# Four sequences side by side in a linear-attention and feed-forward kernel: order of chunks, 64-token halves from the start, a new opening order, and the branch's registers

## The chip, the cores and the metric

One core of one Trainium2 chip. The metric is the device time of one execution in microseconds (us). The kernel before was timed three times: 488.36, 488.54 and 982.09 us; the median, 488.54 us, is the figure that the change is measured against. One further execution was profiled; it took 487.69 us, of which the trace covers a span of 485.9 us.

The engines are called by their short names in the profile: PE is the matrix engine (PEld is its weight load), DVE the vector engine, ACT the scalar engine, POOL the general-purpose engine (GpSimd), SP the engine whose queue issues most DMAs.

## The reference, cut to what matters

Two stages, chained. The first is a linear attention with a per-channel decay over 4 batches, 8 heads, 768 tokens and a head width of 48:

```python
state = np.zeros((B, H, D, D))
for t in range(S):
    cur = np.einsum('bhd,bhe->bhde', u[None] * kt, vt)
    y[:, :, t] = np.einsum('bhd,bhde->bhe', rt, state + cur)
    state = wt[:, :, :, None] * state + np.einsum('bhd,bhe->bhde', kt, vt)
```

The second takes the 3072 tokens (4 x 768) with 384 features each through a feed-forward layer of width 2048: `h = x @ w_in`, `g = h * sigmoid(1.702 h)`, `out = g @ w_out`, in float32. The four batches have nothing to do with each other; within a batch the state goes from token to token.

## The kernel before, in words

**Chunks.** The tokens are cut into 24 chunks of 128 (`NT`), six per batch, and taken in the order of memory: chunks 0 to 5 are batch 0, 6 to 11 batch 1, and so on. `chunk(t)` (line 406) is a generator that does one chunk in steps; each step is called for by a token of an order written by hand. In a chunk two prefix products of the decays are made by scans on DVE (L419, L425), r*k for the diagonal (L432), the scaled k and r (`kf`, `qf`, L440, L441); PE makes the diagonal terms `ps_d` (L448) and transposes `kf` (L474, or L468 later). The state of the chunk before is scaled on DVE (L459). Then, for chunks 0 to 5, the whole 128 x 128 chunk is done at once: the matrix `am` with the diagonal on it is written by ACT (L494, eight instructions), PE makes the state's update (L505, added on DVE in L511), the scores (L523) and the state's share of the output (L530; L568 in chunk 3), DVE puts the scores above the diagonal into `am` (L574), and PE multiplies with the values (L617; L613 in chunk 3). From chunk 6 on (`HALF`) `token_halves` (L316) does two halves of 64 tokens with an intermediate state `mid`: half the score columns, `am` by L349, the states by L354 to L359, L361 for the scores. There the matmuls are of 64 rows or columns, and `one_run` (L285) emits those of one chunk's outputs together with the scores and sums of the next chunk (`held`), except for the chunks in `ALONE`, 6 and 8, whose scores and sums run by themselves. The first chunk of a batch has no incoming state, the last makes no outgoing one.

**x.** The output of a chunk is written as a rounded high part by ACT and a remainder. For chunks 0 to 3 the remainder is made by a matmul with the matrix `minus` (L635) and an ACT copy (L636); later by DVE (L246). Rows of x are moved between partitions by `fill_x` (L645), six DMAs per group; of the first group, three chunks are moved so and chunk 3 is computed in the moved layout (L568, L613, with POOL copies L556, L562).

**Feed-forward.** Groups of four chunks (512 tokens); each group has 16 tasks, one per 128 columns of the width 2048, in all 96. A task is a first product (token `g`: nine matmuls), a gelu (`h`: two ACT instructions, one DVE subtraction, L693) and a second product (`y`: nine matmuls). The first 20 tasks use all 128 rows at once (L677, L707 to L709); tasks 20 to 94 are split by rows in two that run side by side (L733). The weights arrive as raw 64-bit words in 12 pieces (`fetch`, token `f`) and are converted in four steps (`convert`, token `w`: ACT L222 and L223; DVE L225 and L228; ACT L231; DVE L233).

**Order.** All engines take their instructions in program order. The first part is the string `RAMP` (L63): `l` loads a chunk, `a` does the next step of a chunk, `f`, `w`, `g`, `h`, `y` as above, `x` moves x, `k13` issues 13 matmuls on zeros (`keep_clock`, L713). `rest()` (L884) makes the order after it from the tables `PARTS`/`LATER`. DMAs are issued from SP's queue in `RAMP` and mostly from POOL's after it.

**End.** After the last task the sums in `acc` are compared with limits (L937 to L945); every engine loads the count (L948) and branches (L949) over a slow version of the whole kernel that runs only if a limit is broken. The output of a group is stored by three DMAs (`store`, L802).

Of the kernel before, what the change touches and what calls it, by code (L numbers as in the profile page):

```python
# [21 lines left out]
P = 128  # L22
# [30 lines left out]
PARTS = [("a", 0, 0), ("a", 1, 0), ("a", 2, 0), ("m", 2, 0), ("a", 2, 1), ("a", 3, 0), ("a", 3, 1), ("a", 5, 1),  # L53
         ("a", 5, 1), ("l", 5, 0), ("l", 5, 0), ("a", 5, 1), ("a", 5, 1), ("a", 8, 1), ("a", 8, 1), ("x", 8, 1)]
# [9 lines left out]
l0 M l0 a0 a0 a0 l0 k13 a0 a0 l1 l1 a0 a0 a1 k4 a0 a1 f2 a1 l1 a0 l2 a0 k1 a1 a1 a1 a1 a2 f2 k3 a0 a0 w2 a1 a1 a2 f0  # L64
a2 k1 a0 a1 a1 l3 l2 a2 a2 a2 k3 a1 a2 l3 a3 f0 a1 a2 a2 a2 w0 a3 f1 a3 a1 k2 a3 a2 f4 a3 w0 a3 k3 a2 a3 a3 a3 l4 a2
w0 a3 a3 a2 a4 f6 w0 a3 w2 x2 a3 w1 w1 k5 a3 k3 g0 f6 w2 g1 l4 w2 a4 h0 g2 f4 a4 w1 w1 h1 g3 w4 h2 w4 f3 a4 a4 a4 f8
y0 w3 f5 l5 g4 w3 h3 m4 l6 w4 a4 y1 w4 a4 w3 a4 g5 a5 w3 y2 a4 h4 a5 l5 a5 h5 y3 g6 w5 w5 m5 y4 a4 a5 w6 w6 h6 f7 w5
w5 w6 a5 w6 a6 g7 f8 w8 a5 y5 l6 w8 h7 g8 g9 w7 y6 a6 a6 a4 w7 a5 y7 w8 w8 a6 f10 h8 f9 u a5 a6 h9 w7 a6 a5 g10 w9
l7 f10 g11 a5 w7 a6 w9 l8 m6 a5 l7 a7 h10 y8 y9 w9 a6 w10 a7 g12 f11 w9 a6 y10 a7 h11 h12 a5 l9 w11 a7 w10 w11 a7 m7
a7 w10 a7 w11 y11 w10 y12 w11 a6 a7 g13 a7 a8 l8 h13 l9 g14 a6 a8 a8 g15 l10 a8 y13 h14 a7 m8 a7 a8 a8 h15 a9 a9 y14  # L70
a8 x7 y15 a8 a9 l10 a8 g16 g17 h16 m9 a9 h17 a9 a9 l11 g18 a9 y16 a10 a8 h18 y17 a9 g19 a10 a10 a8 a10 a9 a10 h19
m10 a10 l11
"""
WIDE = 512
CROSS = 6
HALF = 6
GAP = 3
ALONE = (HALF, 8)
# [10 lines left out]
def rwkv_ffn_kernel(ctx: ExitStack, tc, wkr, vp, vrk, ub, w_in, w_out, masks, vt, uc, out):  # L89
# [13 lines left out]

    hm = cp.tile([R2, 2 + H], F32, name="hm")
# [11 lines left out]
    after = cp.tile([P, C], F32, name="after")  # L116
# [31 lines left out]
    states = [at.tile([R2, TOP + NP * D], F32, tag=f"sf{i}", name="sf") for i in range(3)]  # L148
# [5 lines left out]
    loaded, state, pools, weighed, moves = {}, {}, {}, set(), []  # L154
# [8 lines left out]
    def load(t):  # L163
# [3 lines left out]
        loaded[t] = [a[0:R2], v]  # L167
        first, last = (TOP if t == 0 else 0), (R2 if t % (NT - 1) == 0 else P)
        rows = wkr.rearrange("t r w -> (t r) w")[t * R + first - TOP : t * R + last - TOP]
# [6 lines left out]
        else:  # L176
            for c0, n_ in ((1, n - 1), (n, NP * C), (n + NP * C, NP * C)):
                one, two = (slice(c0 + h * n_ // 2, c0 + (h + 1) * n_ // 2) for h in range(2))
                behind_moves(queue[0].dma_start(a[TOP:R2, one], wkr[t, :, one]))  # L179
                for h in range(2):  # L180
                    rows = slice(TOP + h * D, TOP + (h + 1) * D)
                    queue[0].dma_start(a[rows, two], wkr[t, (1 - h) * D : (2 - h) * D, two])  # L182
        yield
        assert t < 3 or t - 3 in weighed
        queue[0].dma_start(v[:, TOP:], vrk[t, :, 0:DM])
        if t >= WHOLE:
            rk = pools["late"].tile([P, 2 * DM], F32, tag="rk", name="rk_t")
            queue[0].dma_start(rk, vrk[t, :, DM:])
# [66 lines left out]
    def decays(t):  # L255
# [3 lines left out]
        queue[0].dma_start(w, wkr[t, :, 0 : n + 1])  # L259
# [793 lines left out]
```

## Time and profile before

| | us |
|---|---|
| median of three runs | 488.54 |
| profiled execution, device time | 487.69 |
| its span in the trace | 485.9 |
| first product's matmuls begin without break | 35.50 |
| last matmul begins | 479.11 |

PE is busy for 475.3 us of the span, 38 of its instructions being the `k` matmuls on zeros, all before 35 us. DVE is busy 60% of the span, ACT 53%, POOL 22%; DVE and ACT are much busier in the first quarter than later. The granted clock of PE is at full speed in every slice of the page but the last, in which no matmul runs. 48.47 MB are moved by DMA, at around 300 GB/s in the first 60 us and far less afterwards. An instruction's time in these views is from its start to its end; neighbours on one engine overlap a little, so where a sum is made along an engine, the distance from start to start counts.

### The profile page before, as it was taken

How to read it: one execution, taken by the hardware profiler on the slowest of the kernel's cores; microseconds unless marked ns; L12 is line 12 of the kernel's file. 1: busy time of each engine (PE TensorE's matmuls, PEld its weight loads, DVE VectorE, ACT ScalarE, POOL GpSimd, SP SyncE). 2: the span in 40 equal slices, each digit the busy share in tenths (PEclk: the TensorE clock that was granted, in tenths of full speed). 3: DMA queues.
4: the chain of work that ended last, by engine and by line, in shares of the span. 5: the costliest groups of instructions: out<-in, count | busy, mean ns of one | idle time of the engine just before them, and what ended most of it. 6: DMA issues, size and time to landing. Idle time of an engine off the chain costs nothing.

```text
span 485.9 us, 14346 instructions
## 1 busy us (share of the span) xinstructions
PE 475.3 (98%) x5915; PEld 405.7 (83%) x5915; DVE 289.6 (60%) x455; ACT 256.7 (53%) x611; POOL 107.5 (22%) x222
## 2 busy tenths in 40 slices
PE   7999999999999999999999999999999999999994
PEld 4768888888888888888888888888888888888873
DVE  7999999998866456556656566656575312121110
ACT  5888898875653534634544545445545432422222
POOL 4151000002232406433407334407200002100000
PEclk9999999999999999999999999999999999999998
DMA  8968954125522305223305234205220001100001
GB/s 298 318 234 308 313 170 152 48 93 145 163 75 74 99 3 132 102 70 109 97 5 148 75 94 115 87 14 131 72 63 2 3 1 34 67 2 1 1 0 71
DMA packets 20728, 48.47 MB, mean 100 GB/s; under 512 B 4816, under 2 KB 10032, under 8 KB 20656
## 3 DMA queue, kind: packets, MB, share of 16 engines
q1 hardware_dynamic: 12128, 26.72, 16.7%
q0 software_dynamic: 8128, 20.24, 14.9%
q8 instruction: 48, 0.79, 0.6%
q10 hardware_dynamic: 400, 0.53, 0.3%
q14 instruction: 24, 0.20, 0.1%
HBM read 40.49 MB, written 4.72 MB: 93 GB/s over the span
## 4 chain that ended last, share of the span: by engine, by line
PE 95%; DVE 2%; DMA 1%; issue 1%; ACT 0%; SPq 0%; ACTq 0%; PEldq 0%; DVEq 0%
PE po L733 31%; PE ph L733 30%; PE ph L677 9%; PE ps_c L293 5%; PE ps_a L293 3%; PE po L707 3%; PE po L709 3%; PE po L708 3%; PE ps_d L448 1%; PE ps_y L617 1%; PE ps_t L474 1%; PE ps_y L530 1%; PE ps_s L523 1%; PE ps_t L468 1%; DMA wkr_t<-in_wkr 1%; PE idle L722 1%
## 5 line engine op out<-in xcount | busy, mean ns | idle before, releaser
L733 PE MATMUL ph<-x,pair 64*128 64x512 f32 x1350 | 220.7, 377 | 0.0
L733 PE MATMUL po<-gh,pair 64*128 64x512 f32 x912 | 186.1, 383 | 0.2 <-SPq L738 0.2
L733 PEld LDWEIGHTS ph<-x,pair 64*128 64x128 f32 x1350 | 170.1, 186 | 17.8 <-ACT gf L692 0.6
L693 DVE TENSOR_TENSOR gl<-gf,gh 128x512 fp32r<-128x512 f32 x96 | 66.2, 691 | 147.8 <-ACT gf L692 147.8
L692 ACT ACTIVATE gh<-ph 128x512 fp32r<-128x512 f32 x84 | 49.9, 594 | 151.3 <-PE ph L733 144.3
L733 PEld LDWEIGHTS po<-gh,pair 64*128 64x128 f32 x912 | 113.5, 186 | 12.6 <-SPq L738 0.8
L733 PE MATMUL po<-gl,pair 64*128 64x512 f32 x456 | 117.1, 376 | 0.0
L733 PEld LDWEIGHTS po<-gl,pair 64*128 64x128 f32 x456 | 58.8, 186 | 5.7
L645 POOL DMA_DIRECT2D x<-x x33 | 16.7, 511 | 169.4 <-DVE x L246 77.1
L692 ACT ACTIVATE gf<-ph 128x512 f32<-128x512 f32 x84 | 49.6, 590 | 0.0
L677 PE MATMUL ph<-x,pair 128*128 128x512 f32 x189 | 45.5, 390 | 0.4 <-DMA x<-x 0.3
L677 PEld LDWEIGHTS ph<-x,pair 128*128 128x128 f32 x189 | 35.0, 188 | 7.9 <-DMA x<-x 1.0
L349 ACT ACTIVATE am<-eye,s 128x64 f32<-128x64 f32 x144 | 36.2, 336 | 3.8 <-PE ps_c L293 3.2
L182 POOL DMA_DIRECT2D wkr_t<-in_wkr x72 | 36.1, 505 | 5.5 <-issue 3.2
L419 DVE TENSOR_TENSOR_SCAN lp<-wkr_t,d1r 112x516 f32<-112x516 f32 x24 | 29.3, 1223 | 1.3 <-DMA wkr_t<-in_wkr 1.2
L246 DVE TENSOR_TENSOR x<-ps_c,x 112x512 fp32r<-112x512 f32 (+1 forms) x20 | 12.6, 638 | 29.2 <-ACT x L245 29.2
L425 DVE TENSOR_TENSOR_SCAN lp<-wkr_t,d1f 112x516 f32<-112x516 f32 x24 | 29.5, 1228 | 0.1
L245 ACT ACTIVATE x<-ps_c 112x512 fp32r<-112x512 f32 (+1 forms) x20 | 11.1, 555 | 29.4 <-PE ps_c L293 29.4
L293 PE MATMUL ps_a<-kq 48*64 48x64 f32 (+1 forms) x576 | 26.3, 221 | 0.0
L707 PE MATMUL po<-gh,pair 128*128 128x512 f32 x60 | 23.7, 396 | 0.0
L179 POOL DMA_DIRECT2D wkr_t<-in_wkr x36 | 18.8, 523 | 22.1 <-DVE lp L425 12.1
L709 PE MATMUL po<-gl,pair 128*128 128x512 f32 x60 | 23.2, 386 | 0.0
(128 smaller groups left out, 654.3 us busy)
## 6 DMA issues: line engine op xcount, KB each, us to landing
raw<-in_w_out SPq DMA_DIRECT2D x6, 1024.0 KB, 7.7
raw<-in_w_in SPq DMA_DIRECT2D x5, 1024.0 KB, 10.1
rk_t<-in_vrk POOLq DMA_DIRECT2D x12, 384.0 KB, 4.5
wkr_t<-in_wkr SPq DMA_DIRECT2D x4, 770.5 KB, 9.0
out_t<-ob POOLq DMA_DIRECT2D x12, 256.0 KB, 2.6
v_t<-in_vrk SPq DMA_DIRECT2D x12, 192.0 KB, 3.5
wkr_t<-in_wkr POOLq DMA_DIRECT2D x24, 96.0 KB, 2.6
wkr_t<-in_wkr POOLq DMA_DIRECT2D x48, 48.0 KB, 2.2
```

What stands on the lines that cost most here:

```text
L179: behind_moves(queue[0].dma_start(a[TOP:R2, one], wkr[t, :, one]))
L182: queue[0].dma_start(a[rows, two], wkr[t, (1 - h) * D : (2 - h) * D, two])
L293: mm = T.matmul(out, w, moving, start=start, stop=stop, skip_group_check=True)
L349: A.activation(am[h][:, p], eye, AF.Copy, scale=s[:, j : j + 1])
L419: V.tensor_tensor_scan(li.rearrange("r p c -> r (p c)")[:, ::-1], w1[:, ::-1], d1r.rearrange("r p c -> r (p c)")[:, ::-1], 0.0, op0=ALU.mu ...
L425: V.tensor_tensor_scan(pm.rearrange("r p c -> r (p c)"), w0, d1f.rearrange("r p c -> r (p c)"), 0.0, op0=ALU.mult, op1=ALU.add,)
L677: T.matmul(o, pair[w_], halves(x[:, x_, c, cs], plain), start=k_ == 0, stop=k_ == 3 * NM - 1)
L692: A.activation(g, ph, AF.Gelu_apprx_sigmoid, scale=1.0 / W_SCALE)
L693: V.tensor_tensor(gl, gf, gh.bitcast(F32), op=ALU.subtract)
L707: T.matmul(o, h_, halves(gh, plain), start=first, stop=False, skip_group_check=True)
L709: T.matmul(o, h_, halves(gl, plain), start=False, stop=f == NF - 1, skip_group_check=True)
L733: mm = T.matmul(by_twos(out), w[rows], halves(x[rows]), start=start, stop=stop, skip_group_check=True)
```

## The change

1. Chunk t now is chunk t // 4 of batch t % 4 (`place(t)` = t % B * CB + t // B): chunks 0 to 3 are the first of each batch, without incoming state; the state of chunk t comes from chunk t - 4; chunks 20 to 23 are the last. There are six state buffers instead of three, handed round by a table.
2. Chunks 0 to 2 go through `token_halves` in an `opening` form: scores in 64-token halves, only the first half's sums, `mid` copied by ACT, one output tile, remainder by PE as before (`by_tensor`). Chunk 3 has its own function `last_rows`. Their outgoing states are made later and separately (`first_state`, token `n`). Chunks 4 and 5 go through `token_halves` too (`CROSS` is 4, `ALONE` is 4 and 8).
3. In chunks 0 to 7 half of the diagonal matrices is written by POOL (`affine_select`) instead of ACT.
4. `RAMP` is another order; it has 33 matmuls on zeros before the first `g` and one after it instead of 38 and none.
5. The sums are compared during task 94, counted at task 95, and each engine loads the count ahead of the last store; the constants `eye` and `later` are made at the start instead of inside `RAMP`. The output of a group is stored as four pieces of 128 tokens per row, 512 bytes each, instead of one of 2 KB.

```diff
+    def place(t):
+        return t % B * CB + t // B
...
-        first, final = t % CB == 0, (t + 1) % CB == 0
+        opening, final = t < B, t >= NT - B
...
-            for b in range(1 if final else 2):
+            for b in range(1 if opening or final else 2):
...
-        if t in ALONE:
+        if opening or t in ALONE:
             one_run([], ahead)
...
+            if h and t < WHOLE:
+                for x in half:
+                    G.affine_select(
+                        out=am[h][x], in_=s[x, h::2].unsqueeze(2).broadcast_to([HB, NP, HB]), pattern=[[0, NP], [1, HB]],
+                        base=0, channel_multiplier=-1, compare_op=ALU.is_equal, fill=0.0,
+                    )
+                continue
...
+        if opening:
+            A.copy(mid[:, TOP:], flat[0])
...
+    def by_tensor(t, y):
...
+        A.activation(hi, y, AF.Copy, accum_out=acc_x[0:n, 2 * t : 2 * t + 1])
+        yield
+        T.matmul(y, minus[0:n, 0:n], hi, start=False, stop=True, skip_group_check=True)
+        A.copy(lo, y)
...
+    def last_rows(t, kf, qf, v, s):
+        am = wide
+        for h in range(2):
+            if h:
+                G.affine_select(
+                    out=am[h], in_=s[:, h::2].unsqueeze(2).broadcast_to([P, NP, C]), pattern=[[0, NP], [1, C]],
...
+                A.activation(am[h][:, p], ident, AF.Copy, scale=s[:, 2 * p + h : 2 * p + h + 1])
+        yield
...
+                T.matmul(ps[h][:, p], kf[head(h), p], qf[head(h), p], start=True, stop=True)
...
+        G.tensor_copy(vz[:, :, TOP : TOP + R], v[:, TOP : TOP + NM * R].rearrange("s (m c) -> s m c", m=NM))
+        G.tensor_copy(vh[:, :, TOP:], three.rearrange("s (m c) -> s m c", m=NM)[:, :, 0:TOP])
+        yield
+        for h in range(2):
+            V.copy_predicated(am[h], after_b, ps[h])
...
+        for n, (out_, w_, x_) in enumerate(each):
+            T.matmul(out_, w_, x_, start=n < 2, stop=False, skip_group_check=True)
...
+    def first_state(t):
+        kf, kt, v = kept.pop(t)
+        if kt is None:
+            kt = transposed(kf)
+            yield
...
+                T.matmul(ps_u[head(h), p], kt[:, p, columns], v[:, c : c + D], start=True, stop=True)
+        yield
+        new = state[t] = states[t]
+        A.copy(new[:, TOP:], ps_u.rearrange("r p d -> r (p d)"))
...
-        if not first:
-            sf = state[t - 1]
+        if t >= B:
+            sf = state[t - B]
...
+                if i == len(TASKS) - 1:
+                    count(counted.pop())
...
+                    if group == len(CHUNKS) - 1:
+                        counted.append(nc.values_load(cnt, min_val=0, max_val=full))
+                    store(group, lambda m: by_batch[m, :, :, group * C : (group + 1) * C], B * C, (1, 0, 2) if kind == "r" else range(NM))
```

The opening's order after the change, up to the first two `g` (before it stands in L64 to L66 of the kernel above):

```
l0 l0 l1 M a0 l1 l0 a0 f1 a0 a1 k14 a0 a0 l1 l2 a1 a1 a0 k3 n0 a0 a1 a0 f0 a0 a2 w1 a2 l3 a1 a0 a2 a1 k3 a1 n0 a1 n1
l2 a2 a1 a3 a3 a0 a2 a2 a0 k4 a2 f0 a2 n2 a1 k1 w0 l3 f2 a3 a2 w0 k2 a3 a2 n2 a3 a1 l4 a3 a3 a1 f2 f4 a3 a3 a2 w0 k1
a2 k1 a3 w0 w2 x2 n3 a3 f3 w1 w2 a4 k3 n3 f5 w1 a3 w2 g0 w2 g1 h0 f4 l4 w1 a4 n3 n1 h1 g2 y0 f6 f8 w3 y1 a4 a4 h2 w4
```

## Rows read from the trace of the kernel before

**Rows 1.** The page, busy time, share of the span and instructions of PE.

```profile
PE 475.3 (98%) x5915; PEld 405.7 (83%) x5915; DVE 289.6 (60%) x455; ACT 256.7 (53%) x611; POOL 107.5 (22%) x222
```

**Rows 2.** Stretches: us, busy time (count) per engine, granted clock, DMA.

```profile
12.00:24.00 12.00, 11.99 (x159) 9.66 (x159) 11.85 (x20) 10.52 (x29) 1.53 (x2) 1.00 1.00 317
132.00:480.00 348.00, 346.77 (x4642) 302.45 (x4640) 166.70 (x286) 153.72 (x387) 87.66 (x170) 1.00 0.21 60
```

**Rows 3.** Chain that ended last, opening: start us, us, what.

```profile
3.77 1.24 DVE lp L419
...
33.50 2.47 DMA x<-x
```

**Rows 4.** PE in order of time: start, us, what, count, [idle before].

```profile
35.50 8.60 PE L677 MATMUL ph<-x,pair 128*128 128x512 f32 x35 [0.26 <-DMA x<-x]
...
51.44 0.67 PE L505 MATMUL ps_u<-v_t,kt 128*64 128x48 f32 x16
52.03 1.16 PE L523 MATMUL ps_s<-kq 64*128 64x128 f32 x16
...
63.57 1.08 PE L530 MATMUL ps_y<-kq,sf 64*64 64x128 f32 x16
64.58 1.09 PE L617 MATMUL ps_y<-am,v_t 128*64 128x128 f32 x16
...
85.65 0.60 PE L293 MATMUL ps_a<-v_t,kt 64*64 64x48 f32 x29
...
102.20 0.27 PE L293 MATMUL ps_c<-kq,sf 64*64 64x64 f32 x2
...
104.35 6.09 PE L677 MATMUL ph<-x,pair 128*128 128x512 f32 x27
```

**Rows 5.** DVE from 0 to 31 us by form: count, busy us, mean ns.

```profile
L574 DVE COPY_PREDICATED am<-after,ps_e 128x512 f32<-128x512 int32 x6 | 4.0, 720 | 0.0
...
L511 DVE TENSOR_TENSOR sf<-ps_u,sf 112x192 f32<-112x192 f32 x3 | 1.1, 351 | 0.0
L459 DVE TENSOR_TENSOR sf<-sf,lp 112x192 f32<-112x192 f32 x3 | 1.0, 342 | 0.0
```

**Rows 6.** DVE, the whole span by form: the 64-token form of L574.

```profile
L361 DVE COPY_PREDICATED am<-later,ps_a 128x256 f32<-128x256 int32 x36 | 15.5, 441 | 3.7 <-ACT am L349 3.4
```

**Rows 7.** ACT in order of time.

```profile
8.22 0.17 ACT L451 COPY s<-ps_d 128x8 f32<-128x8 f32 x1 [3.65 <-PE ps_d L448]
...
13.74 2.45 ACT L494 ACTIVATE am<-ident,s 128x128 f32<-128x128 f32 x8
...
16.66 1.16 ACT L222 ACTIVATE raw<-raw 128x1024 int32<-128x1024 uint32 x1
...
18.85 0.56 ACT L636 CAST x<-ps_y 112x512 fp32r<-112x512 f32 x1
...
31.44 0.59 ACT L636 CAST x<-ps_y 112x512 fp32r<-112x512 f32 x1 [0.75 <-PE ps_y L635]
...
88.78 2.03 ACT L349 ACTIVATE am<-eye,s 128x64 f32<-128x64 f32 x8 [0.55 <-PE ps_y L617]
```

**Rows 8.** DVE in order of time.

```profile
26.83 1.22 DVE L225 SCALAR_TENSOR_TENSOR raw<-raw 128x1024 int32<-128x1024 int32 x1
28.09 1.23 DVE L228 SCALAR_TENSOR_TENSOR c<-c,raw 128x1024 int32<-128x1024 int32 x1
...
103.28 2.34 DVE L233 TENSOR_TENSOR pair<-c,pair 128x1024 fp32r<-128x1024 f32 x2
```

**Rows 9.** POOL in order of time.

```profile
2.67 0.29 POOL L118 TENSOR_SCALAR_AFFINE_SELECT after<-after 128x128 f32<-128x128 f32 x1
...
27.05 1.18 POOL L556 COPY spare<-sf 112x144 f32<-112x144 f32 x1 [3.45 <-DVE sf L459]
```

**Rows 10.** ACT's queue at the end, by line: count, ns, start us.

```profile
L948 ACTq TENSOR_LOAD <-acc x1: 642/642/642, 481.1 to 481.1; - x1
...
L949 ACTq EVENT_SEMAPHORE x1: 17/17/17, 484.9 to 484.9; - x1
```

More of the change, by code (lines that the diff above doesn't have):

```diff
@@ L152, in rwkv_ffn_kernel @@
     V.memset(lands[0][0:TOP], 1.0)
-    loaded, state, pools, weighed, moves = {}, {}, {}, set(), []
+    loaded, state, pools, weighed, moves, kept = {}, {}, {}, set(), [], {}
+    free, mids, news = list(range(B, STATES)), {}, {}
+    for t in range(B, NT):
+        mids[t] = free.pop(0)
+        news[t] = free.pop(0) if t < NT - B else None
+        free += [news.get(t - B, t - B), mids[t]]
+    def place(t):
+        return t % B * CB + t // B
     def behind_moves(dma):
@@ L390, in token_halves @@
                             c = (2 * p + o) * D
-                            add(b, o, p, b, v[half[b], c + o * TOP : c + HB], am[o ^ p // 2][half[b], p])
-        one_run(here, held.pop() if held else None)
+                            add(b, o, p, b, v[half[b], c + o * TOP : c + HB], am[swapped(p, o)][half[b], p])
+        one_run(here, held.pop() if held and not opening else None)
         weighed.add(t)
         yield
+        if opening:
+            yield from by_tensor(t, whole)
+            return
         cols = slice(col * C, (col + 1) * C)
@@ L461, in chunk @@
         yield
[L462 to L475 removed]
+        kt = transposed(kf) if t != CROSS - 1 else None
@@ L496, in update @@
-        def update():
-            if final:
-                return
-            ps_u = ps_a.tile([R2, NP, D], F32, tag="psa", name="ps_u")
-            for p in range(NP):
-                for h in range(2):
-                    c = name(p, h) * D
-                    T.matmul(ps_u[head(h), p], kt[:, p, head(h)], v[:, TOP + c : TOP + c + D], start=True, stop=True)
-            new = state[t] = states[t % 2]
-            flat = ps_u.rearrange("r p d -> r (p d)")
-            if sf is None:
-                A.copy(new[:, TOP:], flat)
-            else:
-                V.tensor_tensor(new[:, TOP:], flat, sf[:, TOP:], op=ALU.add)
@@ L513, in chunk @@
-        for part in (update, diagonal) if steady else (diagonal, update):
-            part()
-            yield
-        if t < CHUNKS[0] - 1:
-            ps = [ps_h.tile([P, NP, C], F32, tag="ph", name=f"ps_e{h}") for h in range(2)]
-        else:
-            ps = [ps_a.tile([P, NP, C], F32, tag="psa", name=f"ps_s{h}") for h in range(2)]
-        for p in range(NP):
-            for h in range(2):
-                T.matmul(ps[h][:, p], kf[head(h), p], qf[head(h), p], start=True, stop=True)
@@ L800, in rows_of, with store @@
             yield
-    def store(i, start, N, order=range(NM)):
+    def store(i, dst, N, order=range(NM)):
         for m in order:
@@ L823, in rwkv_ffn_kernel @@
         where = [(i, col) for i, n in enumerate(CHUNKS) for col in range(n)]
-        starts = [sum(CHUNKS[:i]) for i in range(len(CHUNKS))]
+        by_batch = out.rearrange("m p (b s) -> m p b s", b=B)
         last = {}
```

361 lines of the change are left out of this document (144 added, 217 removed).

## The prediction

> **What bounds the kernel now.** I read the page's busy times first: PE 98% of the span, DVE 60%, ACT 53% [rows 1]. A share over the whole span says little here, so next the stretches: from 132 to 480 us PE is idle for 0.7 us of 347.5 (its last matmul ends at 479.5) and DVE for half of it, so there the matmuls alone set the time; from 12 to 24 us DVE is busy 11.85 of 12.00 us and PE's 11.99 are no proof of need, since part of them is matmuls on zeros [rows 2]. Third, the chain of waits from the front: a scan on DVE at 3.77 us opens it, and the DMA that moves x (33.50 + 2.47) closes the opening [rows 3]. Fourth, PE in order of time: the first product runs without break from 35.50, released by that DMA; one of its matmuls went ahead, so the work on the path begins at about 35.3 [rows 4]. So the time is the opening (35.3), then what PE has to do until 479.5, then a tail. A part of the change counts if it moves the start of the first product, takes matmuls out after it, makes PE wait for weights, or shortens the tail.
>
> **The opening on DVE.** A chunk costs DVE two scans and three products; that stays. What goes in chunks 0 to 3: three scalings of the state (342 ns each) and three additions (351), 2.1 us by their length; and for chunks 0 to 2 six predicated copies of 720 ns become six of 441, 1.7 us [rows 5, 6]. Neighbours overlap by about 0.1 us, so 3.0 us rather than 3.8. Put in the new order, DVE's work up to the scores of chunk 3 is then some 24 us from 3.77, to 27.5, where it was done at 30.8. That alone would bring the first product to about 32.3.
>
> **The opening on ACT.** DVE isn't all. ACT's start-to-start costs: a w's first step 2.19 us (16.66 to 18.85), eight diagonals of 128 columns 2.45, of 64 columns 2.03, a rounded x or its remainder 0.5 to 0.6, a small copy 0.17 [rows 7]. New on ACT: three copies of `mid` and three or four of first states at about 0.25 each (between the 0.17 and the 0.5 of the rows), 1.7 us. Gone: half of the diagonals, and the others of half width; per chunk 2.45 falls to 1.0 (0.25 each), for chunk 3 to 1.2, 5.6 us in all. I list ACT's queue from the first small copy at 8.22 to chunk 3's remainder, the last thing the first product needs: diagonals 4.2, copies of s 0.5, four transposed k 1.8, states 1.7, seven roundings and remainders up to it 3.9, three first steps of w at 2.2, three later at 1.05: about 22.5 us, to 30.8 if ACT never waits. It waits: for chunk 1's transposes, which now stand on PE behind chunk 0's output, and for PE's diagonal of chunk 3; I find 2.4 us. So chunk 2's remainder, after which x is moved, is done at about 29.2 (it was done at 32.03 [rows 7]), the moves are in 3.5 us later as before, at 32.7, chunk 3's x is rounded at 32.5, PE makes its remainder's matmul (0.5), and the first product starts at **33.2**: 2.1 us gained. Bounds: 31 without any wait, 35.3 if hand-overs between engines, which the list takes without latency, eat the gain.
>
> **The loads.** SP's queue keeps its order l2, f0, l3 with the wait of f0's second part for its first in the middle; bytes ahead of chunk 2 are as before, those ahead of chunk 3's scan leave it at most 0.6 us late, in a stretch where DVE later waits longer for the scores. Costed at nothing; if it were on the path, 0.6.
>
> **PE after the first product.** Chunks 4 and 5 were done whole. Chunk 4: update 0.6, scores 1.1, state 1.0, values 1.0, and chunk 5, which had no outgoing state, the same without the update and without transposes, 6.8 us in all; then chunk 6's scores and sums ran alone, 1.0 (from 85.65) [rows 4]. After: chunk 4's scores alone 1.0, then two runs that carry one chunk's output beside the next one's scores, 2.15 each by the run from 102.20 to 104.35, and 0.4 for chunk 5's transposes: 5.7 against 7.8, **2.1 us** gained. Against that: one matmul on zeros, 0.2. Later chunks: 32 sums are now saved at the ends of batches where it was 40 sums and state products, 8 matmuls at 2.15 / 64, 0.3 us lost. The state updates of the first chunks all stand before the first product in PE's order, so they cost nothing after it; their cover is the wait for x.
>
> **Weights.** DVE has to follow. Before, the conversion of the piece used by task 13 ended at 105.62 (103.28 + 2.34), its first half near 104.45, and task 13's matmuls began at 104.35 [rows 4, 8]: no slack. My sum of DVE's queue to that point falls by 6 us, PE's start of task 13 by about 4, so the slack grows to 2 us there; but the first two second products now come before the fourth task, and their weights are ready within half a microsecond of the need. I take 0.5 us of waits, between 0 and 2.
>
> **POOL instead of ACT.** Two `affine_select` per chunk, for seven chunks, and a bigger one for chunk 3. On an idle chip a select of 128 x 128 took 0.29 us; a copy of 112 x 144, issued while DVE worked, took 1.18 and ended 0.18 us after DVE's instruction did (28.05), and DVE's next one started at 28.09, on time [rows 8, 9]. So I let POOL be late, up to 1.2 us an instruction, which the order covers except for chunk 3, and DVE not at all. The Trainium skill ("SBUF — State Buffer", Who interferes with whom) has it that a vector instruction with two SBUF inputs and a GpSimd one that reads SBUF exclude each other, whichever comes second waiting in full; the trace shows POOL waiting (1.18 us), no run here shows DVE doing so. By that rule POOL's longer selects could hold DVE too; what that makes of the time is the first rival.
>
> **State, stores, tail.** The state's chain is four chunks long instead of one; no wait for a state stands on PE's path in the long stretch [rows 2], so that gains nothing. Stores in pieces of 512 bytes load POOL's queue a little, with nothing waiting; the last three are on SP and ACT, where each issue could grow: 0 to 0.3 us each for the two on ACT. The tail: ACT loads the count at 481.1 for 0.64 us, branches, and is at the other side at 484.9 [rows 10]. Loaded ahead, while ACT waits for the last matmuls, this takes 0.8 us out (0.64 and the semaphore in front); the 3 us after the branch stay. Net 0.6, between 0 and 0.8.
>
> **Sum.** 2.1 + 2.1 - 0.2 - 0.3 - 0.5 + 0.6 = 3.8 us less: profiled 487.7 would become 483.9; the median stands 0.85 higher, so 488.54 becomes **484.7**.
>
> **Rivals.** *POOL holds DVE.* Place: the selects of chunks 0 to 7. Price: a select of 256 columns runs some 0.45 us by itself (an estimate from the 0.29 for 128 columns), at most the 1.18 of the copy. There are 7 in the opening, where DVE otherwise waits 1.3 us for chunk 3's scores, and 8 after it, with 2 us of slack: 0.45 gives 1.8 + 1.6, so 488.1; 1.18 gives 7.0 + 7.4, so 499. For: POOL and DVE visibly meet. Against: DVE's on-time start at 28.09. This is the rule of the Trainium skill's page above, taken for the side that the trace doesn't show. It turns the sign from about 0.5 us a select on. Chance 0.15, most of it near 488. *The opening isn't shorter*: engines hand over more often, ACT gets no idle time, the first product stays at 35.3; then 484.7 + 2.1 = 486.8, or 487.5 if the waits for weights double. For: some ten hand-overs from chunk 0 to chunk 3; against: DVE's 3 us are plainly gone. Chance 0.2. *More than that*: the opening at ACT's bare sum, 31, no waits for weights: 484.7 - 2.2 - 0.5 = 482. For: the slack on DVE; chance 0.17. *The load ahead does nothing*, since the far side of the branch is what comes late, and the longer issues cost 0.6: 485.9; it sits inside the forecast's width.
>
> **How the numbers follow.** The forecast, 483 to 486.3, has 0.48. With the rivals' times and the bounds (waits 0 to 2, opening 31 to 35.3, tail) the range is 481 to 488.6. A measurement of this kernel tells about 2% (9.8 us) from no change: below 478.8 all gains would have to be doubled, 0.05; above 498.3 only POOL's highest price leads, 0.04; the rest, 0.91, lies within.
>
> **What would show it.** Right: first product near 33.2 without break; no PE gap over 0.3 us before task 13; DVE's predicated copies at 441; ACT's count loaded before 479. Wrong: DVE instructions starting late beside a select of POOL; ACT idle before chunk 3's rounding; matmuls waiting for `pair`; PE's granted clock below full speed in the opening, which has fewer matmuls on zeros and more gaps.

## The result and the profile after

The changed kernel is slower. Over eleven runs of each, its median is 494.38 us against 490.04 for the kernel before, a ratio of 1.0083 [1.0054, 1.0113]; the bracket is a 95% interval, so 0.8% is little but clear of no change. Ratios and intervals, here and below, go by the fast runs of each kernel and not by all of them (982.09 us is one that is left out), so they are not the quotients of the medians. The forecast was 484.7, from 481.0 to 488.6. The profiled execution took 493.93 us with a span of 492.2; by the sum it should have taken 483.9. These 10.0 us are what has to be found. From here on, line numbers are those of the changed kernel.

The first view is PE in order of time: start, length, line, what, and in brackets the idle time before it and what ended it.

```profile
40.33 6.65 PE L634 MATMUL ph<-x,pair 128*128 128x512 f32 x27
...
64.66 0.60 PE L310 MATMUL ps_a<-v_t,kt 64*64 64x48 f32 x29 [0.56 <-ACT kt L511]
...
122.58 0.89 PE L634 MATMUL ph<-x,pair 128*128 128x512 f32 x3
124.24 0.89 PE L634 MATMUL ph<-x,pair 128*128 128x512 f32 x3 [0.78 <-DMA x<-x]
125.29 2.83 PE L634 MATMUL ph<-x,pair 128*128 128x512 f32 x12 [0.16 <-DMA x<-x]
...
485.46 0.38 PE L666 MATMUL po<-gl,pair 128*128 128x512 f32 x1
```

Three points cut the time into the forecast's three pieces. The first product starts at 40.33 (before: 35.3 [rows 4]; forecast: 33.2). From there to the last matmul it takes 445.1 us (before 479.11 - 35.3 = 443.8; forecast 443.8 - 2.1 + 0.2 + 0.3 + 0.5 = 442.7), and the lines at 122 to 125 show PE stopping for the moves of the second group's x. From the last matmul to the span's end it takes 6.74 (before 6.8; forecast 6.2). The misses are 7.1, 2.4 and 0.5: together the 10.0. So the place to look is the opening.

Stretches of the changed kernel: length, busy time (count) of PE, PEld, DVE, ACT, POOL, then PE's granted clock, DMA's share and GB/s.

```profile
11.00:12.00 1.00, 0.51 (x11) 0.37 (x8) 1.00 (x2) 0.55 (x2) 0.18 (x1) 1.00 1.00 394
12.00:18.00 6.00, 5.80 (x63) 4.41 (x62) 3.88 (x7) 2.98 (x8) 0.82 (x2) 0.62 0.99 322
18.00:24.00 6.00, 6.00 (x78) 5.34 (x77) 4.61 (x9) 1.94 (x9) 0.62 (x2) 0.50 0.42 122
24.00:30.00 6.00, 5.83 (x117) 4.10 (x116) 2.97 (x4) 4.58 (x11) 1.30 (x1) 0.74 0.90 264
132.00:480.00 348.00, 347.57 (x4777) 303.05 (x4777) 173.89 (x300) 155.61 (x395) 91.48 (x172) 1.00 0.24 64
```

From 12 to 24 us DVE was busy 11.85 of 12.00 us [rows 2]; now it is busy 3.88 and 4.61 of 6. PE's granted clock, at full speed there before, is 0.50 (1.2 instead of 2.4 GHz) from 18 to 24. DMA, which also never paused, has a hole: 122 GB/s. The last row answers to [rows 2] as well; PE is busy throughout there, as before: the long stretch has nothing to do with it.

What DVE waits for, in order of time (the two r*k products, L557, are for the POOL rival below):

```profile
15.72 1.23 DVE L544 TENSOR_TENSOR_SCAN lp<-wkr_t,d1r 112x516 f32<-112x516 f32 x1 [2.05 <-DMA wkr_t<-in_wkr]
...
18.35 0.67 DVE L557 TENSOR_TENSOR rku<-wkr_t 112x512 f32<-112x512 f32 x1
...
22.38 1.23 DVE L544 TENSOR_TENSOR_SCAN lp<-wkr_t,d1r 112x516 f32<-112x516 f32 x1 [1.01 <-DMA wkr_t<-in_wkr]
...
25.01 0.83 DVE L557 TENSOR_TENSOR rku<-wkr_t 112x512 f32<-112x512 f32 x1
28.86 0.69 DVE L565 TENSOR_TENSOR kq<-wkr_t,lp 112x512 f32<-112x512 f32 x1 [3.03 <-PE ps_y L310]
...
35.20 1.36 DVE L480 COPY_PREDICATED spare<-spare,ps_s 128x512 f32<-128x512 int32 x2 [1.92 <-PE ps_s L474]
```

Four waits, 8.0 us. Two are for the loads of chunks 2 and 3. One is a buffer: `kq` has two, so chunk 3's scaled k has to wait until chunk 1's output matmuls have read theirs, and those stand on PE behind chunk 2's scores. One is for chunk 3's scores. The clock did not wait for them: taken microsecond by microsecond, it falls in this trace at about 13.5, just before the first of these waits begins (13.67). The loads come from SP's queue (start, length of the issue):

```profile
8.24 0.33 SPq L192 DMA_DIRECT2D wkr_t<-in_wkr  x1
8.61 0.43 SPq L220 DMA_DIRECT2D raw<-in_w_in  x1
9.08 0.43 SPq L221 DMA_DIRECT2D raw<-in_w_in  x1
13.01 0.33 SPq L192 DMA_DIRECT2D wkr_t<-in_wkr  x1
...
19.93 0.34 SPq L226 DMA_DIRECT2D raw<-in_w_in  x1
```

The first weight's two DMAs, 960 KB, go out 0.4 and 0.8 us behind chunk 2's load of 770 KB, and share the engines with it. The queue then stands until 19.93, where the weight's last part may be sent: that is the hole in the DMA row. The same queue in the kernel before, with an earlier weight piece's load ahead of chunk 2's:

```profile
3.16 0.43 SPq L207 DMA_DIRECT2D raw<-in_w_in  x1
...
8.36 0.33 SPq L175 DMA_DIRECT2D wkr_t<-in_wkr  x1
10.94 0.34 SPq L209 DMA_DIRECT2D raw<-in_w_in  x1
11.33 0.41 SPq L203 DMA_DIRECT2D raw<-in_w_in  x1
11.79 0.42 SPq L204 DMA_DIRECT2D raw<-in_w_in  x1
12.96 0.35 SPq L175 DMA_DIRECT2D wkr_t<-in_wkr  x1
```

There the first weight's two big parts (L203, L204) left 3.0 and 3.4 us behind chunk 2's load (8.36). Between them, at 10.94, stands the second part of another piece, the second `f2` of the order before. It waited for that piece's first part, sent at 3.16, which landed 7.7 us later, and the queue stood for 2.2 us. The changed order takes `f1` first, a single DMA, so nothing stands between chunk 2's load and the weight.

What came as forecast: DVE's copies of 64-token halves in the opening take 437 ns, as in [rows 6].

```profile
L394 DVE COPY_PREDICATED am<-later,ps_e 128x256 f32<-128x256 int32 x6 | 2.3, 437 | 0.3 <-ACT sf L387 0.3
```

### The profile page after: what moved, and what is told of

Same layout as the page of the kernel before. It is cut to its first block, busy times and chain, and to the rows that moved or that the text cites. A ratio compares the mean times of both kernels' runs of the same rounds, so it can differ in the third digit from the quotient of the medians.

```text
span 492.2 us, 14974 instructions
## 1 busy us (share of the span) xinstructions
PE 479.9 (98%) x6226; PEld 408.5 (83%) x6226; DVE 288.9 (59%) x454; ACT 249.4 (51%) x586; POOL 117.4 (24%) x232
## 4 chain that ended last, share of the span: by engine, by line
PE 84%; DMA 5%; DVE 5%; ACT 1%; issue 1%; SPq 1%; POOL 1%; ACTq 0%; PEldq 0%; DVEq 0%; POOLq 0%
PE po L690 31%; PE ph L690 30%; PE ps_c L310 6%; PE ph L634 5%; PE ps_a L310 3%; DMA raw<-in_w_in 3%; DMA x<-x 1%; PE ps_y L310 1%; PE po L664 1%; PE po L666 1%; PE po L665 1%; PE ps_d L573 1%; PE ps_t L510 1%; PE idle L679 1%; PE ps_e L310 1%
## 5 line engine op out<-in xcount | busy, mean ns | idle before, releaser
L382 ACT ACTIVATE am<-eye,s 128x64 f32<-128x64 f32 x156 | 39.6, 339 | 0.5 <-PE ps_c L310 0.5
L199 POOL DMA_DIRECT2D wkr_t<-in_wkr x72 | 37.1, 532 | 6.3 <-issue 2.9
L375 POOL TENSOR_SCALAR_AFFINE_SELECT am<-s 64x256 f32<-64x256 f32 x14 | 12.0, 860 | 77.4 <-PE ps_c L310 31.5
L263 DVE TENSOR_TENSOR x<-ps_c,x 112x512 fp32r<-112x512 f32 (+1 forms) x22 | 13.9, 640 | 28.0 <-ACT x L262 28.0
L310 PE MATMUL ps_a<-kq 48*64 48x64 f32 (+1 forms) x640 | 29.5, 221 | 0.0
L262 ACT ACTIVATE x<-ps_c 112x512 fp32r<-112x512 f32 (+1 forms) x22 | 12.3, 559 | 31.2 <-PE ps_c L310 31.2
L310 PEld LDWEIGHTS ps_c<-kq,sf 64*64 64x64 f32 (+3 forms) x640 | 20.8, 127 | 7.3 <-issue 6.0
L310 PE MATMUL ps_c<-kq,sf 64*64 64x64 f32 (+3 forms) x640 | 26.3, 223 | 0.4 <-PEq L327 0.4
```

What stands on the lines that cost most here:

```text
L199: queue[0].dma_start(a[rows, two], wkr[q, (1 - h) * D : (2 - h) * D, two])
L262: A.activation(hi, f, AF.Copy, accum_out=acc_x[0 : f.shape[0], to : to + 1])
L263: V.tensor_tensor(lo, f, hi.bitcast(F32), op=ALU.subtract)
L310: mm = T.matmul(out, w, moving, start=start, stop=stop, skip_group_check=True)
L382: A.activation(am[h][:, p], eye, AF.Copy, scale=s[:, j : j + 1])
```

## The experiments

Theory after this reading: the opening is late because the weight's load is put right behind chunk 2's (**load**); rivals: the clock's fall is the cause and would be cured by matmuls on zeros (**clock**), POOL's selects hold DVE (**POOL**), the reuse of `kq` and PE's order hold it anyway (**order**). Behind the first product, the second group's x (**x**); at the end, the store's 512-byte pieces (**store**). The edits for load, clock, order and x change the order string alone, those for POOL and the store the code; `k3` is three matmuls on zeros, `f0` the first weight's load, `l3` that of chunk 3. The numbers, with the changed kernel's above them:

| kernel | median, us | ratio to the kernel before | first product | to the last matmul | mean clock of that trace |
|---|---|---|---|---|---|
| changed | 494.38 | 1.0083 [1.0054, 1.0113] | 40.33 | 445.1 | 0.982 |
| e1 zeros | 495.42 | 1.0165 [1.0131, 1.0199] | 41.48 | 443.5 | 0.987 |
| e2 load order | 491.12 | 1.0051 [1.0002, 1.0100] | 35.80 | 445.4 | 0.993 |
| e3 no selects on POOL | 493.12 | 1.0104 [1.0060, 1.0148] | 39.43 | 444.4 | 0.992 |
| e4 whole rows stored | 493.35 | 1.0060 [1.0010, 1.0109] | 40.30 | 444.9 | 0.983 |
| e5 = e1 + e2 | 489.70 | 1.0021 [0.9996, 1.0046] | 35.68 | 444.6 | 0.998 |
| e6 = e2 + order | 490.31 | 1.0018 [0.9990, 1.0046] | 36.49 | 444.7 | 0.998 |
| e7 second x | 492.60 | 1.0047 [1.0009, 1.0085] | 44.76 | 442.8 | 0.977 |
| e8 = e6 + e7 | 490.72 | 1.0028 [1.0001, 1.0055] | 37.23 | 444.7 | 0.988 |
| e9 = e5 + e7 + more order | 489.59 | 1.0025 [0.9996, 1.0053] | 34.95 | 444.8 | 0.996 |
| e10 late count | 492.57 (one run) | - | 38.27 | 444.4 | 0.992 |
| e11 = e5 + e7 | 488.93 | 1.0007 [0.9976, 1.0038] | 36.43 | 443.9 | 0.995 |
| e12 = e9, rounding later | 491.53 | 1.0057 [1.0028, 1.0087] | 35.89 | 446.4 | 0.992 |

The ratio is to the runs of the kernel before on the same chip; the experiments ran on four chips, so rows are to be compared by it and not by the medians. The start, the stretch and the mean clock are from one traced execution each; that of e7 was one of its longest runs (497.44 us), which matters below.

**Zeros alone (e1).** Nine more matmuls on zeros, load order as changed. (The changed order has 32 of them ahead of the first `g`, and 33 in all; with the nine it is 41 ahead, against 38 in the kernel before.)

```diff
-... k3 n0 a0 a1 a0 f0 a0 a2 w1 a2 l3 a1 a0 a2 a1 k3 a1 n0 a1 n1
+... k3 n0 a0 k2 a1 k3 a0 f0 a0 a2 w1 a2 l3 a1 a0 a2 a1 k3 a1 n0 a1 n1 k4
```

> The changed kernel with nine more matmuls on zeros in the opening (two before and three after chunk 1's diagonal, four after chunk 1's state update), in places where PE otherwise waited; nothing else. Clock theory (PE fell to 1.2 GHz from 13.7 to 27.1 us because the opening in halves gives it too little to do between 9.5 and 13.7 us, and the slow matmuls lengthen the chain): the clock stays at full speed, the first product starts 3 to 5 us earlier than at 40.3, the time falls by 3 to 5 us against the changed kernel. Load theory (chunks 2 and 3 arrive late, 2.05 and 1.0 us of waits on DVE, and the slow clock lies beside those waits): the clock stays up, but the first product moves by less than 1.5 us. POOL theory: no move.

The first product came at 41.48, later than before the edit. The clock was full up to 24 us, fell in the stretch from 24 to 30 and was low in the next. The same view of e1:

```profile
18.00:24.00 6.00, 5.96 (x110) 4.47 (x109) 5.21 (x9) 3.91 (x12) 1.65 (x2) 1.00 0.80 282
24.00:30.00 6.00, 4.27 (x63) 3.65 (x62) 4.94 (x7) 1.81 (x6) 0.00 (x0) 0.85 0.79 224
30.00:36.00 6.00, 5.83 (x67) 4.85 (x65) 0.14 (x1) 3.99 (x11) 1.17 (x3) 0.50 0.20 76
```

PE was busy 4.27 of the 6 us in which the clock fell; one stop, of 1.56 us at 27.03, is put down to nothing that the profile shows. Chunk 3's scores then took 2.08 us at the lower level where they take 1.16 at the higher (in e5). So in this trace the fall came later and was not avoided. The ratio, 1.0165, lies above that of the changed kernel, with the intervals apart: zeros alone cost time.

**Load order alone (e2).** The weight goes out behind chunk 3's load.

```diff
-... n0 a0 a1 a0 f0 a0 a2 w1 a2 l3 a1 a0 ...
+... n0 a0 a1 a0 a0 a2 w1 a2 l3 f0 a1 a0 ...
```

> The changed kernel with the first piece of weights of the first product issued behind chunk 3's load instead of ahead of it; nothing else. Load theory: DVE's waits for chunk 2 (2.05 us) and chunk 3 (1.0) vanish, the first product starts 2 to 3 us earlier than at 40.3. Clock theory: the scans start earlier, the clock falls all the same, and the first product moves by less than 1.5 us.

The first product starts 4.5 us earlier. DVE's waits of this run:

```profile
14.12 1.23 DVE L544 TENSOR_TENSOR_SCAN lp<-wkr_t,d1r 112x516 f32<-112x516 f32 x1 [0.54 <-DMA wkr_t<-in_wkr]
...
24.36 0.69 DVE L565 TENSOR_TENSOR kq<-wkr_t,lp 112x512 f32<-112x512 f32 x1 [0.93 <-PE ps_y L310]
...
30.68 1.36 DVE L480 COPY_PREDICATED spare<-spare,ps_s 128x512 f32<-128x512 int32 x2 [0.70 <-PE ps_s L474]
```

All four shrink, also those that no load ends: 2.05 to 0.54, 3.03 to 0.93, 1.92 to 0.70, and the wait for chunk 3's load is gone; two for ACT's middle copies, 0.46 and 0.81 us, stand out now. How the load reaches the others is argued and not shown step by step: r*k late, PE's diagonal late, chunk 1's output later, chunk 3's k later. The clock was lower for 3.4 us in this trace (from 14.6 on), for 13.7 in that of the changed kernel, and is a part of the difference. The ratio falls from 1.0083 to 1.0051 only, with intervals that overlap, and the tail of this trace is 1.6 us longer (8.30 against 6.74).

**Both (e5).** The edits of e1 and e2.

> The first two edits together: the first weight load goes out behind the loads of chunks 2 and 3, and nine more matmuls on zeros stand in the opening. With the load order alone the first product started at 35.80 us and the granted clock still stood at 0.50 from 14.6 to 18 us, in which VectorE lost 0.5 us to a late load and 0.46 us to the fourth's copy. If the load order is the cause and the low clock beside it costs little, the first product starts at 35.3 to 35.8 and the time is that of the load order alone (1.005 times before). If the low clock has a price of its own, the matmuls of 14.6 to 18 us take half as long, the first product starts at 34.3 or earlier, and the time is 1 to 1.5 us below it. If nine matmuls on zeros are only work on TensorE, as the first experiment suggests, the first product comes later than 35.8, by up to 2 us.

The clock is 1.00 in every stretch of the opening, and the first product starts at 35.68, as with the load order alone, but stops after one matmul:

```profile
35.68 0.40 PE L634 MATMUL ph<-x,pair 128*128 128x512 f32 x1
36.62 6.29 PE L634 MATMUL ph<-x,pair 128*128 128x512 f32 x26 [0.55 <-DMA x<-x]
```

So between these two traces the 3.4 us of low clock that e2 still had cost the start nothing to speak of. The time came as the second case had it, 1.5 us below e2's by the ratios, but the intervals overlap. The ratio, 1.0021, is the first whose interval holds 1.

The cleanest test of the load order is e1 beside e5: both have the nine zeros, and the place of `f0` is the only difference. The first product comes at 41.48 and 35.68, the ratio is 1.0165 [1.0131, 1.0199] and 1.0021 [0.9996, 1.0046]. So that the load's place costs time is shown by the runs themselves. Whether it does so by DVE's waits or through the clock, which is higher in e5 too, they don't separate.

**What the clock costs (e7 and e10 beside the changed kernel).** These two change nothing ahead of the first product, nor does e4; the four openings are the same program. Yet the first product starts at 40.33, 44.76, 38.27 and, in e4, 40.30. Stretches of e10:

```profile
12.00:18.00 6.00, 5.82 (x130) 4.79 (x127) 4.80 (x8) 4.56 (x13) 1.65 (x2) 1.00 1.02 325
18.00:24.00 6.00, 3.91 (x41) 2.33 (x39) 5.53 (x9) 2.89 (x10) 2.17 (x2) 0.83 0.78 258
24.00:30.00 6.00, 5.83 (x135) 5.21 (x130) 3.17 (x6) 2.82 (x7) 0.02 (x1) 0.89 0.55 130
```

Of e7:

```profile
18.00:24.00 6.00, 3.30 (x45) 2.34 (x42) 4.29 (x7) 2.75 (x10) 0.82 (x2) 0.83 0.64 194
24.00:30.00 6.00, 5.83 (x107) 5.05 (x100) 4.60 (x9) 2.69 (x5) 0.00 (x0) 0.50 0.81 239
30.00:36.00 6.00, 5.83 (x60) 5.08 (x58) 1.96 (x2) 1.92 (x7) 1.17 (x3) 0.50 0.47 171
36.00:42.00 6.00, 6.00 (x38) 4.06 (x39) 3.45 (x4) 4.65 (x7) 1.56 (x3) 0.50 0.07 15
```

In both, PE waited for DVE after 18 us, for 2.09 us in e10 and 1.26 in e7, and the clock fell at 22; in e10 it was back before 26, in e7 only after 42. Counting the missing share of each stretch, PE lost 1.7 us of full clock in e10, 6.8 in the traces of the changed kernel and e4, and 10.0 in e7, and the first product follows in that order. So the changed kernel's opening is an unsteady one: the same program starts 6.5 us apart. Part of its lateness is there without much of the clock: e2 lost 1.7 us too and starts at 35.80, e10 at 38.27. How much of the 6.5 us is the clock alone stays open, since the loads land at other times too.

The record also gives the mean granted clock of every run, and the times go with it. Beside the experiments the kernel before ran 86 times, at 0.990 to 0.999, median 0.996 or above on each chip; five of these runs, at 0.990 and 0.991, took 491.6 to 492.9 us. Ten of the eleven runs of the changed kernel lie at 0.977 to 0.987, and one, at 0.989, took 489.66. With e4 and e7, whose openings are the same and which save a microsecond or so elsewhere, eight runs lie from 0.989 to 0.991; they took 488.6 to 491.8. So at one mean clock the changed kernel does not show as the slower one. A straight line through the runs gives 0.4 us more for each 0.001 of mean clock less, in either kernel; from 0.996 to the changed kernel's average of 0.983 that is some 5 us, an estimate, where 0.8% is 4 us. All of the loss can lie with the clock. That the clock is its cause is not shown, since a late load makes PE wait as well and the two come together. The edits that win the time back bring the clock back too, to 0.996 on average in e5 and in e11.

**POOL (e3).** All diagonals written by ACT.

```diff
-            if h and t < WHOLE:
+            if False:
...
-            if h:
+            if False:
```

> The changed kernel with all diagonals written by ACT, none by POOL. POOL theory (the selects, 860 ns each on average and 1.72 us for chunk 3, hold DVE or the copies that need them): the first product starts at least 1 us earlier. Clock and load theories: it starts at 40.3 or later by up to 2 us, since ACT has 1.0 us more to do in each of the first chunks.

The first product starts at 39.43, inside the spread that the changed opening shows by itself, and the ratio, 1.0104, is no lower than the changed kernel's. In the changed kernel, DVE's r*k of chunk 3 takes 0.83 us where chunk 2's takes 0.67 (the DVE rows above); the selects on POOL:

```profile
14.15 0.87 POOL L375 TENSOR_SCALAR_AFFINE_SELECT am<-s 64x256 f32<-64x256 f32 x2 [2.97 <-ACT s L576]
23.33 1.97 POOL L375 TENSOR_SCALAR_AFFINE_SELECT am<-s 64x256 f32<-64x256 f32 x2 [8.30 <-ACT s L576]
```

A pair takes 0.87 us while DVE stands idle (13.7 to 15.7), 1.97 beside DVE's work; it ends at 25.30, inside the long r*k. POOL pays over 1 us, DVE 0.16 us a pair. The rival's point of decision was 0.5 us a select; it is refuted. The Trainium skill ("SBUF — State Buffer", Who interferes with whom) has the one that comes second wait in full; the trace agrees for POOL, whose second select of that pair takes 1.44 us beside a scan. For DVE it doesn't speak against it: the r*k at 25.01 came when 0.29 us of the select were left.

**Order in the opening (e6).** On top of e2, chunk 1's output ahead of chunk 2's scores and the first rounding behind the middle copy.

```diff
-l2 a2 a1 a3 a3 a0 a2 a2 a0 k4 a2 f0 a2 n2 a1 k1 w0 l3 f2 a3 a2 w0 k2 ...
+l2 a2 a1 a3 a3 a0 a2 a2 a0 a1 k4 a2 f0 a2 n2 k1 l3 f2 a3 a2 w0 w0 k2 ...
```

> The load order mended, and beside it two moves in the opening: chunk 1's output matmuls go to TensorE ahead of chunk 2's scores, and ScalarE's first part of the second weight's rounding goes behind chunk 2's middle copy. With the load order alone VectorE still waited 0.93 us at 24.36 for chunk 1's output, which holds the buffer that chunk 3's k and r are scaled into, and 0.81 us at 26.52 for the middle copy, which stood behind a rounding that waited 1.02 us for its data. If these reuses and queue places are what is left of the lateness, both waits go, and the first product starts at about 34.3 us instead of 35.8, the time 1 to 1.5 us below that of the load order alone. If chunk 2's scores, which now stand behind 2 us of output matmuls, are late in their place, the first product stays at 35.5 or later.

DVE's wait for `kq` is gone, chunk 3's scores are copied at 29.55 instead of 30.68, and the first product still comes later, at 36.49: PE stands 1.30 us for chunk 3's transposed k, whose copy on ACT is behind a rounding that waits 1.31 us for a weight.

```profile
32.30 1.20 ACT L239 ACTIVATE raw<-raw 128x1024 int32<-128x1024 uint32 x1 [1.31 <-DMA raw<-in_w_in]
...
34.49 0.55 ACT L511 COPY kt<-ps_t 128x448 f32<-128x448 f32 x1
```

The second case's number, 35.5 or later, was met, but not for its reason: the waits went, chunk 2's scores held nobody up, and the next wait stood behind them.

**The second group's x (e7).** Chunk 7's output and rounding ahead of the last first product of the first group.

```diff
-... h13 a6 w11 g15 l8 w11 h14 a7 l8 l9 a7 a8 ...
+... h13 a6 w11 a7 g15 l8 w11 a7 h14 l8 l9 a8 ...
```

> The changed kernel with chunk 7's output matmuls and its rounding moved ahead of the last first product of the first group, so that the six moves of the second group's x begin some 2.7 us earlier. In the changed kernel TensorE waits for them by 1.5 to 3.7 us at the first products of the second group (122 to 124 us). If that wait is a stop of TensorE that is paid in full, the stretch from the first product to the last matmul falls from 445.5 to some 443.5 us and the time by 1.5 to 2 us; the first product stays at 40.3. If the stop is only where TensorE's slack of this stage shows, the wait moves elsewhere (to weights or to a later x) and the stretch stays within 0.5 us.

One wait of 0.48 us is left, and the stretch takes 442.8. Not all of these 2.4 us are the x: with a first product at 44.76, in one of the two longest of ten runs, the weights are ready earlier in proportion. The cleaner pair is e5 and e11, where the same edit takes the stretch from 444.6 to 443.9, in one trace each.

**All orders, then everything (e8, e11, e9, e12).** e8 has the edits of e2, e6 and e7; e11 those of e5 and e7. e9 has the order of e6 and the zeros too, fewer where PE is needed, chunk 2's x moved ahead of a weight's rounding, and the third weight's rounding behind chunk 3's transpose; e12 puts that rounding later still.

```diff
-... a3 a3 a2 w0 k1 a2 k1 a3 w0 w2 x2 n3 a3 f3 w1 w2 a4 k3 n3 f5 w1 a3 w2 g0
+... a3 a3 a2 k1 a2 x2 w0 k1 a3 w0 n3 a3 w2 f3 w1 w2 a4 k3 n3 f5 w1 a3 w2 g0
```

That is e9; e12 ends `... n3 a3 f3 w1 k3 a3 w2 n3 f5 w1 w2 a4 w2 g0`.

> The three mends together: loads of chunks 2 and 3 ahead of the weights, chunk 1's output ahead of chunk 2's scores with the rounding behind the middle copy, and the second group's x earlier. If they are independent causes, the first product starts at about 34.3 us, the stretch behind it takes 443.5 to 444, and the time is 487 to 488.5 us, that is just below the kernel before (0.995 to 0.999 of it). If they hide one another, or the reuse is not what holds VectorE, the time stays at that of the load order alone, 1.003 to 1.006 of the kernel before.

> Load order, matmuls on zeros and the second group's x together, nothing else moved. Load order and zeros gave a first product at 35.68 us and 444.6 us from there to the last matmul, with 1.17 us of waits for the second group's x; the x alone cut that stretch from 445.1 to 442.8 us. If the two add up, the first product stays at 35.7, the stretch takes 442.8 to 443.5, and the time is 0.998 to 1.001 of the kernel before. If the earlier x only gives back what the clock takes, the stretch stays at 444.5 and the time at 1.002.

> Everything that the runs so far point to, in one kernel: loads of chunks 2 and 3 ahead of the weights, the added matmuls on zeros, chunk 1's output ahead of chunk 2's scores, both halves of the second weight's first rounding behind the middle copy, chunk 2's x moved before that weight's copy, the third weight's rounding behind chunk 3's transpose and rounding, and the second group's x earlier. If these waits are separate links of one chain, chunk 2's x leaves at about 29 to 30 us instead of 32.0, the first product starts at 34 to 34.5, the stretch behind it takes 443 us, and the time is 486.5 to 488, that is 0.995 to 0.998 of the kernel before. If the weights' own rounding (VectorE and ScalarE are busy with it from 26 us on) holds the first product, it stays at 35.5, and the time is that of the next kernel, where only the load order, the zeros and the second group's x are changed.

> The kernel with everything mended, and ScalarE's second part of chunk 3's rounding ahead of the third weight's first rounding, not behind it. In the kernel before this one the first product started at 34.95 us but stopped three times for 0.23 to 0.33 us, the last time at 37.56 for that second part, which ScalarE only wrote at 37.04; from the first product to the last matmul it took 444.8 us where the earlier x alone had given 442.8 to 443.9. If these stops are what it lost, the first product still starts at 34.9 to 35.1 us, the stretch falls to 443.3 to 443.9, and the time is 0.998 to 1.000 of the kernel before. If the weights' rounding, which is now later, stops the second product in their place, the stretch stays at 444.8 and the time at 1.0025.

e8 fell short: 37.23, and the clock at 0.54 and 0.60 from 38 to 42, after PE had been busy 0.99 of the 2 us from 34 to 36. e11 came as its first case had it in time, with the best ratio of all; its start was 0.7 later and its stretch 0.4 above the 443.5. e9 has the earliest first product, 34.95, and gives it back at once:

```profile
34.95 0.89 PE L634 MATMUL ph<-x,pair 128*128 128x512 f32 x2 [0.28 <-DMA x<-x]
36.07 1.16 PE L634 MATMUL ph<-x,pair 128*128 128x512 f32 x4 [0.23 <-DMA x<-x]
37.56 3.06 PE L634 MATMUL ph<-x,pair 128*128 128x512 f32 x12 [0.33 <-ACT x L455]
40.89 2.35 PE L634 MATMUL ph<-x,pair 128*128 128x512 f32 x9 [0.27 <-ACT gf L645]
```

e12 removes these stops and gets a worse one, the case that its text names second but larger: PE waits 2.19 us at 42.73 for a gelu, and the clock is at 0.64 and 0.51 from 42 to 46. Between 26 and 42 us DVE is busy 13.3 and ACT 13.0 of the 16 us of e9, so little is left to move, and each edit picks which of them is late. None of the twelve is faster than the kernel before.

**The end (e4 and e10).** e4 stores rows of 2 KB, so that its output has the tokens in the order of the chunks. e10 loads the count after the last store, as the kernel before did.

```diff
-store(group, lambda m: by_batch[m, :, :, group * C : (group + 1) * C], B * C, ...
+store(group, lambda m: by_group[m, :, group], B * C, ...
```

> The changed kernel with the groups of the output stored in rows of 2 KB, as before the change; the output then stands in the order of the chunks, not of the batches. If the 512-byte pieces take back what loading the count ahead gives: the issues of the last stores fall from about 0.6 to 0.35 us, the end comes 0.6 to 1.5 us sooner after the last matmul (6.4 us after its start of 0.38 in both kernels now). If not: the end stays 6.4 us behind.

```diff
-                        counted.append(nc.values_load(cnt, min_val=0, max_val=full))
...
-    n = counted[0]
+    n = nc.values_load(cnt, min_val=0, max_val=full)
```

> The changed kernel with the load of the branch's count put back behind the last store; everything before the last matmul is as in the changed kernel. There the last matmul started 6.74 us before the end of the span, in the kernel before 6.80. If loading ahead takes 0.6 to 0.8 us out of the tail and the longer issues of the stores put it back, this kernel's tail is 7.3 to 7.5 us. If the load ahead does nothing since the stores' landings come last anyway, it stays at 6.7 to 6.8.

The queues' last events in the changed kernel, by line: count, ns, first to last start.

```profile
L854 ACTq TENSOR_LOAD <-acc x1: 486/486/486, 482.1 to 482.1; - x1
...
L911 SPq EVENT_SEMAPHORE  x8: 17/17/17, 489.1 to 490.5; - x8
...
L911 ACTq EVENT_SEMAPHORE  x1: 17/17/17, 488.3 to 488.3; - x1
```

And in e10:

```profile
L908 ACTq TENSOR_LOAD <-acc x1: 839/839/839, 485.1 to 485.1; - x1
...
L909 SPq EVENT_SEMAPHORE  x8: 17/17/17, 486.3 to 489.2; - x8
...
L909 ACTq EVENT_SEMAPHORE  x1: 17/17/17, 486.5 to 486.5; - x1
```

Before, ACT came last, at 484.9 [rows 10]. Now SP does: it waits for the stores to land, and ACT is done 2.2 us earlier, in e10 2.7 earlier even with the late count. So the load ahead is off the path. With 2-KB rows (e4) the end comes 6.00 us after the last matmul's start, with 512-byte pieces 6.74 (6.74 to 8.30 in the twelve traces that have them): the issues on ACT take 0.34 to 0.37 us instead of 0.55 to 0.64, the landing 2.7 instead of 3.3 (median). e10's own tail, 8.24 us, says nothing against it: e7 and e9, which have the count ahead, have 8.19 and 8.28. What makes a tail 6.7 or 8.2 long was not found.

## Why the prediction was wrong

- **The step that failed is the loads**, "Costed at nothing". The prediction has SP's queue keep "its order l2, f0, l3"; it overlooked that in the kernel before `f2`'s second part stood between l2 and f0 and held the queue for 2.2 us. Without it the weight's load follows chunk 2's by 0.4 us where it followed by 3.0 before, so DVE waits 2.05 and 1.01 us, not "at most 0.6". Undoing that order alone takes the first product from 41.48 to 35.68 and the ratio from 1.0165 to 1.0021 (e1 and e5, with the zeros in both), and in one trace each from 40.33 to 35.80 without the zeros (e2).
- **The clock** stood in the last paragraph as a sign of error and in no sum: a term put at nothing, though the prediction itself names "fewer matmuls on zeros and more gaps". It should have been a rival with a price, PE's work of the opening at half speed. The same opening came out between 38.27 and 44.76 with 1.7 to 10.0 us of clock lost, and over the runs of both kernels a lower mean clock goes with a longer time, by enough to cover the whole 0.8%. How the lateness divides between the load's own waits and the clock stays open.
- **The opening on ACT** had the work about right and the waits wrong. Its terms add up to 21.9 us, not 22.5. The views below run from 8.22 to the end of chunk 3's remainder, in the changed kernel and in e5, with ACT's busy time in the fourth place after the length:

```profile
8.22:41.50 33.28, 32.02 (x462) 24.39 (x462) 24.62 (x33) 20.87 (x52) 8.93 (x12) 0.79 0.65 211
8.22:36.85 28.63, 27.30 (x472) 20.33 (x471) 24.93 (x33) 20.83 (x52) 10.14 (x12) 1.00 0.77 247
```

  ACT was busy 20.9 and 20.8 us and idle 12.4 and 7.8, where the prediction says "I find 2.4 us". So with loads mended and the clock full, 35.7 is still 2.5 later than 33.2, and no earlier than the kernel before. The list has no line for `kq`, whose reuse ties chunk 3's DVE work to chunk 1's output on PE (1.30 us in e5), nor for scores that come late on PE (1.20). The bound of 35.3, "if hand-overs between engines, which the list takes without latency, eat the gain", was the better forecast: DVE's copies did become shorter (437 ns), and the gain went into waiting between engines.
- **PE after the first product**: the 2.1 us on chunks 4 and 5 is consistent with the 442.8 of e7, but no run has it alone. The 0.5 for waits was put on weights; the wait was for the second group's x (0.94 us in PE's rows, 1.4 by the starts, since three matmuls that need 0.65 us stand 1.66 and 1.05 apart) and for a transposed k (0.56). When PE's work shrinks, what comes from the side is late next, and I had asked that of weights only.
- **The tail**: the load ahead is there, and the rival *the load ahead does nothing* was right in its result but not for its reason: the store's landing is what comes late, and the tail with 512-byte pieces is 0.7 us longer. The 3 us that the prediction kept behind ACT's branch were not there: 0.5 in the changed kernel, and as little in e10, where the count is loaded late.
- *POOL holds DVE* had the right sign by luck: a pair of selects costs DVE 0.16 us, and without them the kernel is no faster (e3).
- *The opening isn't shorter*, 486.8, was the nearest of the rivals in its mechanism; even this was 7.6 us short, since the opening became longer.

## What to carry to other kernels

When a change moves a transfer in a queue, look up what stands in the queue just ahead of it and how far, and price the sharing: here 2.6 us of distance between a load that the path needs and one that it doesn't was worth 2.5 to 5.8 us of the first product's start in pairs of traces, together with what the clock did in them. It was kept by a wait that had nothing to do with either load, and a new order took that wait away. An opening in which engines hand over often has to be summed along every buffer that is used again, not along its busiest engine; a wait taken out of it shows the next one. And where matmuls on zeros and gaps change, a lower granted clock is a rival with a price, and makes the time of one program spread; compare runs at the same mean clock before naming another cause.

## Not expected of the hardware

The same opening in three traces: granted clock at 0.50 for about 3, 14 and 20 us. Before it fell, PE had been idle for 0.5 us between 11 and 12 in the changed kernel, whose clock fell at 13.5, and for 2.09 and 1.26 us after 18 in e10 and e7, whose clock fell at 22. In e2 it fell at 14.6 with PE idle for 0.15 us of that microsecond and none of the four before, and in e5, idle for 0.17 us there, it didn't. A select pair of 64 x 256 on POOL took 0.87 us beside an idle DVE and 1.97 beside a busy one, while the DVE instruction at its end took 0.83 where it takes 0.67 without. And ACT's event behind the branch came 3.1 us after it in the kernel before (481.8, 484.9), 0.5 us after it in the changed kernel (487.8, 488.3) and in e10 (486.0, 486.5), with nothing in the edits that explains it.
